# A gated linear attention with a feed-forward block: VectorE's transposes of k and q write pairs of tokens into a buffer of another order

## The chip, the cores and the metric

The kernel runs on one core of a Trainium2 chip. The metric is the device time of one execution in microseconds; the time before is the median of three runs, 610.28 us (609.24 to 611.36). A core has TensorE (matmuls, profile names PE and PEld for the weight loads), VectorE (DVE), ScalarE (ACT), GpSimd (POOL) and SyncE (SP), whose queue issues most DMAs here.

## The reference

The attention keeps a 48x48 state per batch and head, which is decayed by a gate, row by row, and takes in the outer product of k and v at each token; the output is q times the state. A SwiGLU block of three matrices follows.

```python
batch, n_heads, seq, head_dim = (4, 8, 768, 48)
...
    f = 1.0 / (1.0 + np.exp(-f_logit))
...
    for t in range(S):
        state = f[:, :, t, :, None] * state + np.einsum('bhd,bhe->bhde', k[:, :, t], v[:, :, t])
        y[:, :, t] = np.einsum('bhd,bhde->bhe', q[:, :, t], state)
...
n_tokens, d_model, d_ff = (3072, 384, 1536)
...
    g = x @ w_gate
    silu = g * (1.0 / (1.0 + np.exp(-g)))
    val = x @ w_val
    return (silu * val @ w_out).astype(np.float32)
```

All inputs are float32 apart from the weights, which come as 64-bit floats and are converted in the first part of the kernel.

## The kernel before

The 768 tokens are cut into six chunks of 128 (C), and a chunk of one batch is a unit u = 4 * chunk + batch, 24 in all. Chunks are counted here from one in words (the third chunk has c = 2 in the code, units 8 to 11) and u from zero. The eight heads stand as four pairs (HP = 4), each pair in 2 x 64 partitions of which 48 are used.

For one unit the generator `attention(u)` does these steps, and each `yield` ends one: the sigmoid of f on ScalarE; f's transpose; k's transpose; a scan over tokens from the end ("tails"); the multiplication of k by the tails (into kT); in six units (14 to 19, "turned") a further transpose of kT into qT's memory and four DMAs of it to a DRAM buffer named turn; the scan from the start ("gates"); q's transpose; its multiplication by the gates (into qT); the score matmuls (sc); the masking of the scores (A) and, in turned units, the load of kt from turn; the decayed state; the output matmuls (y); the state's update. In the third to sixth chunks (c >= SQUARES, which is 2) the transposes are VectorE's, in blocks of 32x32. Its input lies in three rooms, one for each of f, k and q, of 800 elements a partition: four DMAs (`load`, lines 426 to 431) bring 32 partitions each, so that a partition holds four tokens (NI = 4) of 48 numbers for each pair of heads. The transposed tokens come out in four runs, one for each i of NI, and `in_turn` writes them where they belong, every fourth element:

```python
    def in_turn(t):

        return t.rearrange("p a (t i) -> p a i t", i=NI)
```

There is one room for each of f, k and q, so `load_after(u)`, which issues the twelve DMAs of the next unit, can fill a room only when VectorE has read it. kT is one tile, qT one of two, gates and tails are one each.

TensorE's work is mostly the feed-forward block of the chunk before: fifteen matmul products per slice of hidden units with sums and differences on VectorE (`mlp_fifteen`), then seven products for the way back (`down_seven`, functions `one` to `seven`). PSUM banks come in kinds A (two banks), B (one), o (two) and b (three). `two` ends with a copy of its B bank to SBUF on ScalarE (line 1082), and `four` then takes the B bank again.

The order on every engine is written out by hand. The table CHAINS gives the step times of each unit, SCORES those of the scores; a loop at the end of `short_path` walks over the blocks of the feed-forward, adds their assumed time to a clock, and lets in every attention step that is due. `in_order` then keeps that order on all engines, SyncE's queue among them. So a DMA instruction that waits holds up all that come after it in SyncE's queue.

For the first three batches of a chunk the output goes to SBUF as yT (line 658), and ten DMAs of SyncE (line 667) put it into xT, the input of the feed-forward. For the fourth batch the state is put into a tile called diagonal (line 543, cleared by GpSimd, filled by ScalarE at line 546). yT and diagonal share one buffer: both have the tag "x".

```python
            yT = att.tile([128, 2, HP // 2 * C], FP32, tag="x", name="yT")
...
                diagonal = att.tile([128, HP, 2 * D], FP32, tag="x", name="diagonal")
                nc.gpsimd.memset(diagonal, 0.0)
```

Of the kernel before, what the change touches and what calls it, by code (L numbers as in the profile page):

```python
# [13 lines left out]
ALU = mybir.AluOpType  # L14
# [275 lines left out]
def short_path(ctx, tc, ident, least, judge, q, k, v, f_logit, moe_w_gate, moe_w_val, moe_w_out, out):  # L290
# [9 lines left out]
    nc = tc.nc  # L300
    B, H, S, D = q.shape
    C = 128
    NCH = S // C
    HP = H // 2
# [6 lines left out]
    N1 = C + 1  # L311
# [3 lines left out]
    SQUARES = 2  # L315
# [47 lines left out]
    def pairs(t, off=0):  # L363
        return t[:, off:off + HP * N1].rearrange("p (a t) -> p a t", t=N1)
# [30 lines left out]
    NI = C // Q  # L395
    RUN = NI * D

    rooms = {}
# [9 lines left out]
    def squares(nm):  # L408
        return rooms[nm][:, Q:Q + HP * RUN].rearrange("t (a i e) -> t a i e", a=HP, i=NI)[:, :, :, 0:Q]

    def in_turn(t):

        return t.rearrange("p a (t i) -> p a i t", i=NI)

    def load(u, what="fkqv"):
        b, c = units[u]
        rows = slice(c * C, (c + 1) * C)
        for nm, src in (("f", f_logit), ("k", k), ("q", q), ("v", v)):
            if nm not in what:
                continue  # L420
            if nm == "v":
                dst = v_of(u)
            elif c < SQUARES:
                dst = raw[nm][u % NRAW]
            else:
                for n in range(4):
                    at = Q * (1 - n % 2)
                    nc.sync.dma_start(
                        out=rooms[nm][Q * n:Q * (n + 1), at:at + HP * RUN].rearrange("t (a e) -> t a e", a=HP),
                        in_=src[b, n // 2::2, rows, :].rearrange("a (t i) d -> t a (i d)", i=NI))  # L430
                continue
            nc.sync.dma_start(out=dst[:, :, 0:D], in_=src[b, :, rows, :].rearrange("h t d -> t h d"))
# [79 lines left out]
    def rows_of(par):  # L512
        return slice(W * par, W * par + D)
# [3 lines left out]
    def bank(name):  # L517
        return banks[-1].tile([128, 512], FP32, tag="a", name=name)
# [10 lines left out]
    def attention(u):  # L529
        b, c = units[u]  # L530
        fr, kr, qr = (raw[nm][u % NRAW] for nm in "fkq")
        v_ = v_of(u)
        gate, tail = (x[u % NROT if c < SQUARES else 0] for x in (gates, tails))

        diagonal = None

        def decay():
            nonlocal diagonal
            if c:
                nc.vector.tensor_tensor(decayed[:, :, 0:D], states[b], whole.broadcast_to((128, HP, D)), ALU.mult)  # L540
            if c and b == B - 1:

                diagonal = att.tile([128, HP, 2 * D], FP32, tag="x", name="diagonal")
                nc.gpsimd.memset(diagonal, 0.0)
                for par in range(2):
                    nc.scalar.copy(diagonal[rows_of(par), :, par * D:(par + 1) * D], decayed[rows_of(par), :, 0:D])

        def transposed(name, src):
            p = bank(name)
            for a in range(HP):  # L550
                nc.tensor.transpose(p[:, a * C:(a + 1) * C],
                                    src[:, 2 * a:2 * a + 2, :].rearrange("t r d -> t (r d)"), ident)
            return p.rearrange("p (a t) -> p a t", t=C)
# [6 lines left out]
        else:  # L560
            p = transposed("fTp", fr)
            nc.scalar.activation(pairs(gate)[:, :, 1:N1], p, AF.Copy if u in ahead else AF.Sigmoid)
        yield
        if c >= SQUARES:
            nc.vector.transpose(in_turn(pairs(gate)[:, :, 1:N1]), squares("f"))
        yield

        kT = att.tile([128, HP, C], FP32, tag="kT", name="kT")
        qT = att.tile([128, HP, C], FP32, tag="qT", name="qT", bufs=2)
        kp, qp = kT, qT  # L570
        if c >= SQUARES:
            nc.vector.transpose(in_turn(kT), squares("k"))
        yield

        n = HP * N1
# [5 lines left out]
        if c < SQUARES:  # L581
            kp = transposed("kTp", kr)
            qp = transposed("qTp", qr)
        nc.vector.tensor_tensor(kT, kp, pairs(tail, 2)[:, :, 0:C], ALU.mult)
        yield
        turned = (SQUARES + 1) * B + 1 < u < (NCH - 1) * B
        if turned:
# [10 lines left out]
        nc.vector.tensor_tensor_scan(gate[:, 0:n], gate[:, 0:n], start, 1.0, op0=ALU.mult, op1=ALU.add)  # L598
        yield
        if c >= SQUARES:  # L600
            nc.vector.transpose(in_turn(qT), squares("q"))
            load_after(u)
        yield
        nc.vector.tensor_tensor(qT, qp, pairs(gate)[:, :, 1:N1], ALU.mult)
        nc.gpsimd.memset(pairs(gate)[:, :, 0:1], 0.0)
        if 0 < c < SQUARES:
            load_after(u)
        if c < SQUARES:
            decay()
# [8 lines left out]
        if c < NCH - 1 and not turned:  # L618
            p = bank("kt")
# [14 lines left out]
        if c >= SQUARES:  # L634
            decay()
# [4 lines left out]
        if c and b < B - 1:  # L640
# [20 lines left out]
            for h in range(H):  # L661
                a, par = h // 2, h % 2
# [31 lines left out]
        if c < NCH - 1:  # L694
            p = bank("dS")
# [13 lines left out]
    def load_after(u):  # L709

        w = u + (1 if units[u][1] >= SQUARES else 2)
        if w < len(units) and (units[w][1] >= SQUARES) == (w == u + 1):
            load(w, "fkqv" if units[w][1] < SQUARES or w == SQUARES * B else "fkq")

    def attention_steps(c):

        runs = [attention(c * B + b) for b in range(B)]
        parts = [3, 6, 3, 3]
        order = sorted((2 * b + s, b, n) for b in range(B) for s, n in enumerate(parts))
        return [lambda b=b, n=n: [next(runs[b]) for _ in range(n)] for _, b, n in order]  # L720
# [445 lines left out]
    mark = traced[-1]  # L1166
    keep_warm(5)
    first = [attention(b) for b in range(B)]
    done = [0] * B

# [82 lines left out]
    for c in range(2, NCH):  # L1253
        for b in range(B):
            run = attention(c * B + b)
            waiting += [((c - 2) * whole + t, lambda run=run: next(run)) for t in times(c)[b]]
# [33 lines left out]
def kernel(  # L1290
# [22 lines left out]
    def judge(bank):  # L1313
# [12 lines left out]
        yield  # L1326

    short_path(tc, ident, least, judge, *args)
    with tc.If(redo[0] > 0):
        general_path(tc, *args)  # L1330
# [32 lines left out]
```

## Time and profile before

| quantity | before |
|---|---|
| median of three runs | 610.28 us |
| the profiled execution | 611.44 us |
| its span | 609.6 us |
| granted TensorE clock, mean | 0.996 |
| from the third chunk's first hidden product (145.7 us) to the fourth's (244.6) | 98.9 us |
| fourth to fifth (340.1) | 95.5 us |
| fifth to sixth (434.1) | 94.0 us |
| sixth chunk's attention, until 523.9 | 89.8 us |

The feed-forward of chunk n runs beside the attention of chunk n + 1; the rows of the table are stretches of the trace between the first hidden products of the blocks. In the lines of the profile, "out<-in" names tiles, x is a count, and after the bar stand the busy time in us, the mean of one in ns, the engine's idle time before them and what ended it. In timeline lines the first number is the start in us from the span's start, the second the length; an engine's name with a q stands for an instruction that its sequencer handles, such as the issue of a DMA.

### The profile page before, as it was taken

The page shows a single profiled execution, that of the slowest core. Times are in us where ns is not written, and L with a number is a line of the kernel's source. Part 1 is how long each engine was busy: PE and PEld are TensorE (multiplying, and loading weights), DVE is VectorE, ACT ScalarE, POOL GpSimd, SP SyncE. Part 2 cuts the span into 40 slices and gives each one's busy share as a digit, 9 for nine tenths or more (in the row PEclk, how much of TensorE's full clock was granted, in tenths as well). Part 3 has the DMA queues.
Part 4 walks back from the last instruction along what each step waited for, and adds up shares of the span by engine and source line. Part 5 has one row for each costly group of instructions (what it writes and reads, how often), then busy time and mean ns, then how long its engine had stood idle before and what let it go on. Part 6 is the DMA issues. An engine that isn't in the chain of part 4 may idle for free.

```text
span 609.6 us, 10796 instructions
## 1 busy us (share of the span) xinstructions
PE 595.8 (98%) x4036; PEld 491.1 (81%) x4036; DVE 494.3 (81%) x833; ACT 288.5 (47%) x554; POOL 7.6 (1%) x52
## 2 busy tenths in 40 slices
PE   7899999999999999999999999999999999999996
PEld 5744545667888799888899988899988899988896
DVE  7999989868999985999996789996878981566731
ACT  3466644313776522476732366742276730366600
POOL 1000000000000000000000000000000000000000
PEclk9999999999999999999999999999999999999999
DMA  9988372005312044323236334145313100100001
GB/s 199 260 194 295 126 247 79 5 15 159 95 39 70 23 108 115 105 53 96 61 89 145 94 97 110 35 112 120 110 44 90 27 6 10 53 1 1 0 1 59
DMA packets 109142, 54.10 MB, mean 89 GB/s; under 512 B 68760, under 2 KB 102168, under 8 KB 109080
## 3 DMA queue, kind: packets, MB, share of 16 engines
q1 hardware_dynamic: 107064, 50.56, 31.3%
q10 hardware_dynamic: 2016, 2.75, 1.2%
q8 instruction: 34, 0.56, 0.4%
q14 instruction: 28, 0.23, 0.1%
HBM read 44.04 MB, written 6.29 MB: 83 GB/s over the span
## 4 chain that ended last, share of the span: by engine, by line
PE 85%; DVE 10%; SPq 1%; issue 1%; DMA 1%; ACT 1%; POOL 0%; DVEq 0%; ACTq 0%; POOLq 0%
PE o L1056 17%; PE A L957 15%; PE B L957 12%; PE gate L755 5%; PE val L755 5%; PE o L957 5%; PE c L957 5%; PE sc L617 4%; PE o L778 3%; PE o L1119 3%; PE y L677 2%; PE y L656 2%; PE dS L697 2%; PE y L652 1%; DVE c L861 1%
## 5 line engine op out<-in xcount | busy, mean ns | idle before, releaser
L1056 PE MATMUL o<-w_out,h 128*128 128x192 f32 x360 | 62.0, 327 | 0.5 <-DVE h L909 0.5
L957 PE MATMUL A<-xs,w_both 128*128 128x256 f32 x240 | 62.1, 381 | 0.0
L1056 PEld LDWEIGHTS o<-w_out,h 128*128 128x128 f32 x360 | 58.7, 190 | 1.7 <-DVE h L909 0.8
L962 ACT COPY c<-A 128x512 f32<-128x512 f32 x40 | 23.3, 583 | 62.6 <-PE A L957 62.6
L962 ACT COPY aside<-A 128x512 f32<-128x512 f32 x60 | 35.1, 584 | 32.6 <-PE A L957 32.6
L858 DVE TENSOR_TENSOR c<-c,aside 128x512 f32<-128x512 f32 x60 | 41.6, 694 | 10.5 <-ACT aside L962 9.0
L957 PEld LDWEIGHTS A<-xs,w_both 128*128 128x128 f32 x240 | 44.9, 190 | 6.5
L909 DVE TENSOR_TENSOR h<-h,c 128x256 f32<-128x256 f32 x100 | 41.1, 419 | 7.3 <-ACT h L973 7.3
L861 DVE TENSOR_TENSOR c<-c,aside 128x512 f32<-128x512 f32 x60 | 41.4, 689 | 2.5 <-ACT aside L962 2.5
L973 ACT ACTIVATE h<-c 128x256 f32<-128x256 f32 x100 | 39.2, 416 | 8.4 <-DVE c L858 5.8
L1056 PE MATMUL o<-ws,h 128*128 128x192 f32 x240 | 41.5, 328 | 0.2 <-DVE A L631 0.2
L957 PE MATMUL B<-xs,w_both 128*128 128x256 f32 x160 | 41.2, 380 | 0.6 <-ACT aside L962 0.6
L957 PE MATMUL c<-xT,w_both 128*128 128x256 f32 x160 | 41.2, 380 | 0.5 <-DVE c L861 0.5
L957 PE MATMUL A<-xs,extra 128*128 128x256 f32 x160 | 41.2, 380 | 0.0
L957 PE MATMUL B<-xT,extra 128*128 128x256 f32 x160 | 41.1, 379 | 0.0
L962 ACT COPY aside<-B 128x512 f32<-128x512 f32 x60 | 35.1, 584 | 11.7 <-PE B L957 7.2
L631 DVE TENSOR_TENSOR A<-sc,causal 128x512 f32<-128x512 f32 x48 | 30.8, 684 | 11.3 <-PE sc L617 11.3
L1056 PEld LDWEIGHTS o<-ws,h 128*128 128x128 f32 x240 | 39.1, 190 | 0.8 <-DVE A L631 0.4
L861 DVE TENSOR_TENSOR c<-o,c 128x512 f32<-128x512 f32 x40 | 27.6, 690 | 10.0 <-ACT h L973 5.8
L957 PEld LDWEIGHTS c<-xT,w_both 128*128 128x128 f32 x160 | 30.3, 190 | 5.0 <-DVE c L861 0.9
L957 PEld LDWEIGHTS B<-xs,w_both 128*128 128x128 f32 x160 | 30.2, 190 | 5.0 <-ACT aside L962 1.0
L957 PEld LDWEIGHTS A<-xs,extra 128*128 128x128 f32 x160 | 30.3, 190 | 4.5 <-ACT c L962 0.4
(138 smaller groups left out, 1140.2 us busy)
## 6 DMA issues: line engine op xcount, KB each, us to landing
fsquares<-in_f_logit_dram SPq DMA_DIRECT2D x64, 96.0 KB, 2.6
ksquares<-in_k_dram SPq DMA_DIRECT2D x64, 96.0 KB, 2.3
qsquares<-in_q_dram SPq DMA_DIRECT2D x64, 96.0 KB, 2.2
v<-in_v_dram SPq DMA_DIRECT2D x24, 192.0 KB, 3.0
w<-in_moe_w_gate_dram SPq DMA_DIRECT2D x6, 768.0 KB, 6.3
w<-in_moe_w_val_dram SPq DMA_DIRECT2D x6, 768.0 KB, 5.1
w<-in_moe_w_out_dram SPq DMA_DIRECT2D x6, 768.0 KB, 5.3
out_dram<-ob ACTq DMA_DIRECT2D x14, 192.0 KB, 2.7
```

The source lines that it names most:

```text
L617: nc.tensor.matmul(sc[par][:, a * C:(a + 1) * C], lhsT=kT[r, a, :], rhs=qT[r, a, :], start=True, stop=True)
L631: nc.vector.tensor_tensor(A[:, par], sc[par].rearrange("p (a t) -> p a t", t=C), causal.unsqueeze(1).broadcast_to((128, HP, C)), ALU.mult)
L755: nc.tensor.matmul(p, lhsT=w[:, j, i, :], rhs=xT[c][:, i, :], start=(i == 0), stop=(i == KT - 1))
L778: nc.tensor.matmul(p, lhsT=hidden_tile(h, n // 2)[:, n % 2 * 2 + b // 2, b % 2 * C:(b % 2 + 1) * C], rhs=w_out[:, j, :], start=(n == 0), s ...
L858: nc.vector.tensor_tensor(dst, a, b, ALU.add)
L861: nc.vector.tensor_tensor(dst, a, b, ALU.subtract)
L909: lagging.append(lambda: f(*args))
L957: nc.tensor.matmul(p[name][:, n, :], lhsT=weights_of[a][:, n, j, :], rhs=tokens[b], start=fresh and n == 0, stop=True, skip_group_check=True)
L962: nc.scalar.copy(t, p[name])
L973: nc.scalar.activation(dst, src[:, 0, :], AF.Silu)
L1056: nc.tensor.matmul(p[:, n, :], lhsT=lhsTs[j][:, n * C:(n + 1) * C], rhs=rhs[:, j, :], start=first and j == order[0] and n == 0, stop=j == ...
L1119: nc.tensor.matmul(p, lhsT=hidden_tile(h, j)[:, 2, n * C:(n + 1) * C], rhs=b22[:, j, :], start=j == order[0], stop=j == order[-1])
```

## The change

From the third chunk on, the transposes of k and q no longer write to every fourth element. With `parted`, the four runs are split in two halves of two: the tokens of a half are interleaved in pairs, so that a run writes every second element, and the halves lie 256 elements apart. As that is not the order of tokens, the transposed k goes into qT's memory and the transposed q into the first 512 columns of k's room, and each multiplication reads from there two neighbours of one half, then two of the other, and writes kT and qT in the order of tokens. f's transpose stays as it was. As k's room is now in use until q's multiplication, `load_after` moves behind that multiplication. The number of instructions is the same.

```diff
+    def split_squares(nm):
+        return squares(nm).rearrange("t a (j i) e -> t a j i e", j=2)
+
...
+    def parted(t):
+
+
+
+        return t.rearrange("p (j a t i) -> p a j i t", j=2, a=HP, i=NI // 2)
...
+        def multiply(out, x, by):
+
+            if c >= SQUARES:
+                for_each = "p a (t j i) -> p a t j i"
+                out, by = (t.rearrange(for_each, j=2, i=NI // 2) for t in (out, by))
+                x = x.rearrange("p (j a t i) -> p a t j i", j=2, a=HP, i=NI // 2)
+            nc.vector.tensor_tensor(out, x, by, ALU.mult)
+
...
         if c >= SQUARES:
-            nc.vector.transpose(in_turn(kT), squares("k"))
+            kp = qT.rearrange("p a t -> p (a t)")
+            nc.vector.transpose(parted(kp), split_squares("k"))
         yield
...
-        nc.vector.tensor_tensor(kT, kp, pairs(tail, 2)[:, :, 0:C], ALU.mult)
+        multiply(kT, kp, pairs(tail, 2)[:, :, 0:C])
         yield
...
         if c >= SQUARES:
-            nc.vector.transpose(in_turn(qT), squares("q"))
-            load_after(u)
-        yield
-        nc.vector.tensor_tensor(qT, qp, pairs(gate)[:, :, 1:N1], ALU.mult)
+            qp = rooms["k"][:, 0:HP * C]
+            nc.vector.transpose(parted(qp), split_squares("q"))
+        yield
+        multiply(qT, qp, pairs(gate)[:, :, 1:N1])
         nc.gpsimd.memset(pairs(gate)[:, :, 0:1], 0.0)
-        if 0 < c < SQUARES:
+        if c:
             load_after(u)
```

## The prediction

> **What bounds the kernel now.** I read the page's busy table first, then the groups by form on VectorE, then the timeline around each place where TensorE pauses, and last SyncE's own timeline, because the change moves loads there.
>
> ```profile
> span 609.6 us, 10796 instructions
> PE 595.8 (98%) x4036; PEld 491.1 (81%) x4036; DVE 494.3 (81%) x833; ACT 288.5 (47%) x554; POOL 7.6 (1%) x52
> ...
> L601 DVE STREAM_TRANSPOSE qT<-qsquares 128x512 f32<-128x512 f32 x16 | 18.0, 1125 | 6.4 <-DMA turn<-qT 6.4
> L572 DVE STREAM_TRANSPOSE kT<-ksquares 128x512 f32<-128x512 f32 x16 | 17.8, 1113 | 0.0
> ...
> L473 DVE SCALAR_TENSOR_TENSOR top<-w,top 128x384 int32<-128x384 int32 x24 | 12.6, 554 | 0.4
> L604 DVE TENSOR_TENSOR qT<-qT,gates 128x512 f32<-128x512 f32 x16 | 11.1, 696 | 0.1
> L584 DVE TENSOR_TENSOR kT<-kT,tails 128x512 f32<-128x512 f32 x16 | 10.8, 674 | 0.0
> ...
> L591 DVE STREAM_TRANSPOSE qT<-kT 128x512 f32<-128x512 f32 x6 | 4.2, 702 | 0.0
> ```
>
> The reader is to see two things. TensorE is busy for 98% of the span, so time saved on VectorE is worth only what it takes out of TensorE's pauses. And the same 128x512 transpose takes 702 ns where it writes neighbours (L591) and 1113 to 1125 ns where it writes every fourth element (L572, L601).
>
> I compared each matmul's start with the one before it, less the usual pitch of that form, from 135 us on. Pauses over 0.2 us that are not a change of matmul shape: 0.72 us at 192.46, 0.64 at 199.25, 0.66 at 208.80, 0.35 at 225.86, 0.45 at 236.17, and 0.31 and 0.24 at 355.6 to 356.1. That is 3.4 us in all, which caps any gain.
>
> The second place is the start of the fifth chunk (u=16, numbering batch-chunk pairs as the code does). SyncE's queue, then the engines that hang on it:
>
> ```profile
> 310.55 1.74 SPq L428 DMA_DIRECT2D qsquares<-in_q_dram  x4
> 313.55 6.81 SPq L667 DMA_DIRECT2D xT<-yT  x10
> 320.46 0.53 SPq L432 DMA_DIRECT2D v<-in_v_dram  x1
> 321.04 0.60 SPq L627 DMA_DIRECT2D kt<-turn  x1
> 321.75 2.61 SPq L594 DMA_DIRECT2D turn<-qT  x4
> ...
> 321.66 0.42 POOL L544 MEMSET diagonal<- 128x384 f32 x1 [8.53 <-DMA xT<-yT]
> ...
> 322.11 0.71 ACT L546 COPY diagonal<-decayed 48x192 f32<-48x192 f32 x2 [8.05 <-POOL diagonal L544]
> 322.84 0.48 ACT L1082 COPY ob<-o 128x384 f32<-128x384 f32 x1
> ...
> 324.87 1.30 PE L1056 MATMUL o<-ws,hs 128*128 128x192 f32 x7
> ```
>
> yT and diagonal share one buffer (tag "x"), so the memset waits until the ten stores of yT have left. ScalarE's copies queue behind it, and the second (L1082) empties the only bank of kind B, which the matmuls at 324.87 take. The copy ends at 323.32, so there is 1.55 us of slack. At the sixth chunk's start the same chain stands at 407.52 (yT), 415.33 (memset), 417.00 (copy done) and 418.85 (matmul): 1.85 us.
>
> [...]L473 reads every second word at 554 ns for 384 elements, in step with L909's 419 ns for 256 and L584's 674 ns for 512, which read neighbours. No row writes at a step of two. [...]the trace shows q's loads leaving at 310.55, as q's transpose ends at 310.52.
>
> **The change part by part.** Durations are from the profiled execution: 611.44 us, of which 609.60 are span, against a median of 610.28.
>
> Transposes: 32 of them. Between 0.70 us (as L591) and 1.11 (no gain); I take 0.70[...]. That is 0.41 to 0.47 each, 13 us of VectorE, mostly where VectorE isn't waited for.
>
> Multiplications: 32, reading pairs from two halves 1 KB apart[...]. Between 0.69 and 1.10[...]. I take 0.69.
>
> Gain in the third chunk. VectorE has no idle time from 177.4 to 207.8, and u=10's k transpose (182.62, 0.41 saved) lies before the pause at 192.46, its q transpose (195.65, 1.17 to 0.70) before that at 199.25. First pause 0.72 to 0.31. The second: TensorE comes 0.41 earlier, VectorE 0.88, so 0.64 to 0.17. The third keeps its 0.66, both being 0.88 earlier; those at 225.86 and 236.17 hang on TensorE's own scores and on the stores. Gain 0.88.
>
> Gain in the fifth chunk. u=17's q transpose waited 3.11 us, until 351.92, for the stores of turn, which read qT. Now it writes into k's room and runs at 348.8; four operations behind it finish by 351.7; only the multiplication waits, to 352.6 instead of 355.4. The 0.31 and 0.24 go. Gain 0.55.
>
> Buffers. qT is written a step earlier, when k is transposed; its last readers are u-2's output matmuls, at least 3.4 us earlier in all units (u=23: 477.04 against 480.40), so no wait. The old wait of k's transpose for the scores of u-1 goes; it cost nothing (0.0 idle at L572).
>
> Loads. load_after comes one step later, and k's room is free only after q's multiplication. Twelve DMAs per unit are concerned. f still leaves after its transpose, with one exception: in u=12 v's load falls between the two steps, so f of u=13 queues behind a v load that needs u=11's matmuls (done 238.89); f lands near 243 instead of 238.3, and the sigmoid with its table load ends before ScalarE is next needed at 245.83. Hidden. k and q now leave back to back after the multiplication, 1.9 us for each four (as 437.28 to 441.04). k is in time everywhere, narrowest at u=16 (lands about 315.9, transposed at 316.95) and u=20 (409.8, 410.93).
>
> What is queued behind them on SyncE pays. For u=15 the multiplication ends at 312.90, less 0.42 for the transpose before it: 312.48. k and q until 316.35, and only then yT, instead of 313.55. Ten stores take 6.2 to 7.3 us; with 6.6 they end at 322.95 instead of 320.36, 2.6 later, and memset, copies and matmuls follow: 2.6 - 1.55 = 1.05 us of new pause. At u=19: multiplication done 406.45, yT at 410.35, end 416.95 instead of 413.78, 3.2 - 1.85 = 1.35. Behind them turn, u=17's f and the sigmoid come some 2.6 us late too, but VectorE next waits for TensorE at 336.44 and ScalarE at 341.21. At the fourth chunk's start k is not later, since SyncE reaches it at 223.05 after the multiplication's end at 222.07; at the end there are no loads. Other yT stores slip by up to 2 us with nobody waiting.
>
> Sum: -0.88 - 0.55 + 1.05 + 1.35 = +0.97 us, 612.4 for the profiled execution, 611.3 on the median.
>
> **Rivals.** Slower: the paired reading costs the multiplications what the transposes gain. Point: L584 and L604. For it: nothing in the profile reads two words here and two 1 KB away. Against: L473[...]. At 1.10 us the third chunk's gain is gone and both load bursts start 0.42 later: 1.05 + 1.35 + 0.84 - 0.55 = +2.7, 613.0. It decides from about 0.9 us on, where +0.2 gives +1.8. Transposes that stay at 1.11 (the change doesn't do what it says) give the same 613.0.
>
> Faster: SyncE's burst is shorter than I think or the chain has more slack, so that the new pauses stay away: -1.43, 608.9. For it: single loads of four take 1.74 us; against: 10 stores alone took 6.26 to 6.81 here.
>
> Late landings: the shifted turn, kt and f loads land late as well and hold scores or ScalarE: 1 to 2 us more, about 612.8. Margins there are 0.5 to 1 us.
>
> **How the numbers follow.** A measurement of this kernel can tell about 0.3%, 1.8 us, from no change. The worked case 0.48 (own range -0.5 to +2.5: 0.33 within, 0.15 slower), paired reading or no transpose gain 0.34 (0.32 slower, 0.02 within), no new pauses 0.12 (0.06 faster, 0.06 within), late landings 0.06 (slower). So 0.06 faster, 0.41 same, 0.53 slower. The time is that of the worked case, 611.3. The range 608.8 to 614.5 runs from the no-pause case to both unknown costs at once.
>
> **What would show it.** Right: L572 and L601 near 700 ns, L584 and L604 near 690; pauses at the u=10 places of about 0.3 and 0.2; k's loads leaving as q's multiplication ends; yT after them; memset of diagonal near 324 and 418; new pauses of about a microsecond ahead of the matmuls on ws,hs. Wrong: transposes over 0.9, multiplications over 0.9, or TensorE unbroken there.

## The result, and the profile after

The changed kernel took 612.57 us (median of 8 runs, 611.96 to 613.92), the kernel before 610.50 on the same chip (8 runs): a ratio of 1.0039 (95% interval 1.0026 to 1.0051). It is a little slower, by about 2 us. Two executions of the runs below, one of the kernel before (770.66 us) and one of the kernel with k last at two places (689.06 us), had granted clocks of 0.75 and 0.85 and are left out of all ratios. The forecast was 611.3 us with a range of 608.8 to 614.5. The profiled execution after the change took 612.67 us, of which 610.94 are span. The profile before had 611.44 and 609.62.

The first two lines are the busy table of the page of the changed kernel, the rest its groups by form on VectorE (count, then busy us and mean ns, then the idle time before them).

```profile
span 610.9 us, 10799 instructions
PE 595.7 (98%) x4036; PEld 490.7 (80%) x4036; DVE 483.1 (79%) x833; ACT 288.0 (47%) x554; POOL 7.6 (1%) x52
...
L590 DVE STREAM_TRANSPOSE qT<-ksquares 128x512 f32<-128x512 f32 x16 | 11.3, 707 | 1.2 <-DMA ksquares<-in_k_dram 1.2
L620 DVE STREAM_TRANSPOSE ksquares<-qsquares 128x512 f32<-128x512 f32 x16 | 11.1, 696 | 0.0
L552 DVE TENSOR_TENSOR qT<-ksquares,gates 128x512 f32<-128x512 f32 x16 | 10.9, 683 | 5.2 <-DMA turn<-qT 5.1
L552 DVE TENSOR_TENSOR kT<-qT,tails 128x512 f32<-128x512 f32 x16 | 10.8, 673 | 0.0
```

VectorE got what it was to get. The 32 transposes fell from 1113 and 1125 ns to 707 and 696, the multiplications stayed at 673 and 683, and VectorE's busy time fell from 494.3 to 483.1 us. TensorE's did not move (595.8 to 595.7), so all of the time lies in its pauses. The wait for turn, 6.4 us in all at q's transpose before, stands at q's multiplication now, with 5.1 us.

To find the pauses I subtracted each matmul's start before from the start of the same matmul after, and noted where the difference steps from one matmul to the next. Both profiles have the same 3.4 us of lowered TensorE clock at 28 us (0.50 granted before and 0.51 after, from 28.0 to 31.4 us), so the steps compare directly:

| matmuls (time after) | step, us |
|---|---|
| B<-xs (192.11) | -0.35 |
| c<-xT (198.50) | -0.40 |
| y<-qT,diagonal (235.10) | -0.36 |
| o<-ws,hs (325.44) | +1.64 |
| scores of u=17 (356.07 to 356.96, all together) | -0.67 |
| o<-ws,hs (420.10) | +1.26 |

At both places on ws,hs the next matmul adds another 0.10; with that and 0.04 of small steps the last matmul starts 1.36 us later than before. Here is the fifth chunk's start in the changed kernel's timeline, engine by engine (start, duration, engine, line, and in brackets the idle time before it and what ended it), the same chain as the one shown before:

```profile
311.46 1.74 SPq L437 DMA_DIRECT2D ksquares<-in_k_dram  x4
313.24 2.82 SPq L437 DMA_DIRECT2D qsquares<-in_q_dram  x4
316.17 6.26 SPq L685 DMA_DIRECT2D xT<-yT  x10
322.53 0.53 SPq L441 DMA_DIRECT2D v<-in_v_dram  x1
...
323.72 0.42 POOL L561 MEMSET diagonal<- 128x384 f32 x1 [12.06 <-DMA xT<-yT]
...
324.17 0.71 ACT L563 COPY diagonal<-decayed 48x192 f32<-48x192 f32 x2 [11.18 <-POOL diagonal L561]
324.91 0.48 ACT L1100 COPY ob<-o 128x384 f32<-128x384 f32 x1
...
325.44 4.17 PE L1074 MATMUL o<-ws,hs 128*128 128x192 f32 x24 [1.47 <-ACT ob L1100]
```

The stores of yT, which began at 313.55 before, now stand behind both bursts of loads and begin at 316.17, though ScalarE had filled yT by 312.90 and TensorE's work stands 1.07 us earlier by then. The memset that needs their buffer runs at 323.72 instead of 321.66, the two copies follow without a gap, and TensorE stands still for 1.47 us until the second copy (L1100) has emptied its bank. The start of the sixth chunk in the same timeline has the same order and the same end:

```profile
406.51 1.74 SPq L437 DMA_DIRECT2D ksquares<-in_k_dram  x4
408.29 1.85 SPq L437 DMA_DIRECT2D qsquares<-in_q_dram  x4
410.25 6.59 SPq L685 DMA_DIRECT2D xT<-yT  x10
...
418.38 0.42 POOL L561 MEMSET diagonal<- 128x384 f32 x1 [11.68 <-DMA xT<-yT]
...
420.10 4.17 PE L1074 MATMUL o<-ws,hs 128*128 128x192 f32 x24 [1.09 <-ACT ob L1100]
```

The gain in the fifth chunk is in VectorE's timeline. The first line is u=17's q transpose in the kernel before, with its wait; the others are of the changed kernel, where the wait for turn stands at u=16's multiplication (330.30) and u=17 has none:

```profile
351.92 1.11 DVE L601 STREAM_TRANSPOSE qT<-qsquares 128x512 f32<-128x512 f32 x1 [3.11 <-DMA turn<-qT]
...
330.30 0.69 DVE L552 TENSOR_TENSOR qT<-ksquares,gates 128x512 f32<-128x512 f32 x1 [5.12 <-DMA turn<-qT]
...
349.40 0.72 DVE L620 STREAM_TRANSPOSE ksquares<-qsquares 128x512 f32<-128x512 f32 x1
...
351.87 0.68 DVE L552 TENSOR_TENSOR qT<-ksquares,gates 128x512 f32<-128x512 f32 x1
```

Before, u=17's q transpose waited until 351.92 for turn to be stored; now it runs at 349.40 and its multiplication is done by 352.55, well ahead of the scores at 356.

### The profile page after: what moved, and what is told of

It reads as the page before. It is cut to its first block, busy times and chain, and to the rows that moved or that the text cites. A ratio compares the mean times of both kernels' runs of the same rounds, so it can differ in the third digit from the quotient of the medians.

```text
span 610.9 us, 10799 instructions
## 1 busy us (share of the span) xinstructions
PE 595.7 (98%) x4036; PEld 490.7 (80%) x4036; DVE 483.1 (79%) x833; ACT 288.0 (47%) x554; POOL 7.6 (1%) x52
## 4 chain that ended last, share of the span: by engine, by line
PE 83%; DVE 9%; SPq 3%; issue 2%; ACT 1%; DMA 1%; POOL 0%; DVEq 0%; POOLq 0%; ACTq 0%
PE A L975 16%; PE o L1074 14%; PE B L975 13%; PE c L975 5%; PE o L975 5%; PE gate L773 5%; PE val L773 5%; PE sc L635 4%; PE o L1137 3%; PE o L796 3%; PE y L695 2%; PE y L674 2%; SPq L685 2%; PE dS L715 2%; SPq L437 1%
## 5 line engine op out<-in xcount | busy, mean ns | idle before, releaser
L876 DVE TENSOR_TENSOR c<-c,o 128x384 f32<-128x384 f32 x15 | 8.3, 550 | 33.4 <-PE o L1074 33.4
```

Source lines behind the costliest of these rows:

```text
L876: nc.vector.tensor_tensor(dst, a, b, ALU.add)
```

## The experiments

The theory (A): the late loads of k and q, issued by u=15 and u=19, push the yT stores of u=14 and u=18 back, and this alone costs time, while the transposes' gain is real and small. The rivals: the paired reading costs the multiplications time (B), or the stores are late for another reason than their place in the queue (F). All kernels compute the whole result. The kernel before had a median of 610.09 us (27 runs) beside the first four experiments and of 610.22 (35 runs) beside the next four. The ratios and their intervals are those of the record; they are not the quotients of the two medians, and differ from them by up to 0.0008.

A profile without the lowered clock at 28 us is 1.36 us shorter for that reason alone. I read that off the steps between before and after_again, whose starts drift by 1.34 us between 28 and 31.6 us and then run level. Of the kernels below none has the dip, so 1.36 us is added to their differences from the profile before. The time after the last matmul's start varies from 5.7 to 6.6 us between profiles whatever the kernel, so differences of traces are taken at that start.

### Only k's transpose in pairs

k keeps the new order. q is transposed as before, in single elements and into qT, and the loads are issued where they were.

```diff
-            qp = rooms["k"][:, 0:HP * C]
-            nc.vector.transpose(parted(qp), split_squares("q"))
+            nc.vector.transpose(in_turn(qT), squares("q"))
+            load_after(u)
         yield
-        multiply(qT, qp, pairs(gate)[:, :, 1:N1])
+        nc.vector.tensor_tensor(qT, qp, pairs(gate)[:, :, 1:N1], ALU.mult)
         nc.gpsimd.memset(pairs(gate)[:, :, 0:1], 0.0)
-        if c:
+        if 0 < c < SQUARES:
             load_after(u)
```

> k alone is transposed in pairs; q's transpose, its multiplication and the place of the loads are those of before. Theory A (the loss is two TensorE pauses ahead of the matmuls on ws,hs, made by the yT stores that queue behind the late k and q loads): no such pauses, the pause near 192.5 us about 0.35 us as after the change, the one near 199.3 still about 0.64, the two of 0.31 and 0.24 near 356 still there; 0.3 to 0.5 us below before, about 610.1 us where before is 610.5. Rival B (the paired pattern itself costs, in the multiplication or in the order on VectorE): slower than before by about half of the change's loss, 611 or more. Rival C (k and q land late and hold VectorE): as theory A, since the loads are early again.

It took 609.43 us, 0.9993 of before (0.9982 to 1.0003). VectorE's groups by form in this kernel:

```profile
L619 DVE STREAM_TRANSPOSE qT<-qsquares 128x512 f32<-128x512 f32 x16 | 18.0, 1123 | 6.0 <-DMA turn<-qT 6.0
...
L590 DVE STREAM_TRANSPOSE qT<-ksquares 128x512 f32<-128x512 f32 x16 | 11.2, 701 | 0.0
L622 DVE TENSOR_TENSOR qT<-qT,gates 128x512 f32<-128x512 f32 x16 | 11.0, 690 | 0.1
L552 DVE TENSOR_TENSOR kT<-qT,tails 128x512 f32<-128x512 f32 x16 | 10.8, 674 | 0.0
```

Both orders stand side by side here: 701 ns where pairs are written, 1123 ns where single elements are, and 674 against 690 ns for the multiplications that read them. B falls. The trace has -0.34 us at the pause at 192 and -0.15 at u=17's scores, and no pause ahead of o<-ws,hs: with the loads in their old place nothing is lost.

### The late loads alone

The buffers and the place of the loads are those of the change, but the transposes write single elements as before.

```diff
-            nc.vector.transpose(parted(kp), split_squares("k"))
+            kp = kp.rearrange("p (a t) -> p a t", a=HP)
+            nc.vector.transpose(in_turn(kp), squares("k"))
...
-            nc.vector.transpose(parted(qp), split_squares("q"))
+            qp = qp.rearrange("p (a t) -> p a t", a=HP)
+            nc.vector.transpose(in_turn(qp), squares("q"))
```

> The buffers, the late loads and the instruction order of the change, but both transposes write every fourth element as before, so no transpose gains. Theory A: k's loads leave another 0.4 us later, pauses ahead of the matmuls on ws,hs of 2.0 and 1.7 us, pauses near 192.5 and 199.3 at 0.7 and 0.6 as before, those near 356 gone: about 3 us above before, 613.5. Rival B: no paired pattern, so no loss, about 610. Rival C: a loss of about 2 us, with idle time of VectorE ended by the loads rather than pauses ended by ScalarE's copy.

It took 614.61 us, 1.0066 (1.0053 to 1.0079): the direction as expected, the size half as large again. Its transposes take 1114 and 1126 ns. TensorE's timeline in this kernel:

```profile
325.33 4.17 PE L1076 MATMUL o<-ws,hs 128*128 128x192 f32 x24 [1.88 <-ACT ob L1102]
...
345.30 0.91 PE L977 MATMUL B<-xT,extra 128*128 128x256 f32 x3 [0.57 <-ACT c L982]
```

The two places ahead of o<-ws,hs cost 2.05 and 1.68 us. What I had not reckoned with is what follows behind the first of them: +0.41 at 339.06 and +0.84 at 345.30, the second where ScalarE's copy is late. Those 1.25 us are the most part of the surprise. So the move of the loads and buffers, without any faster transpose, costs about 4.3 us by the trace (2.92 + 1.36), and the faster transposes of the change take back 2 to 3 of them. The scores of u=17 gain their 0.67 us here too, with transposes of 1.1 us: that gain comes from q's new place in memory and not from the pairs, while the gains of the third chunk, at 192 and 199 us, are missing here and so come from the pairs.

### Single elements read back

Can the transposes write neighbours and the multiplications collect single elements? Four runs of 512 bytes, each with a quarter of the tokens of all four pairs of heads, take the place of the pairs. Two outcomes are set against each other: that the multiplications now lose what the transposes gain (613.5 us), or that they keep their time (612.5).

```diff
     def split_squares(nm):
-        return squares(nm).rearrange("t a (j i) e -> t a j i e", j=2)
+        return squares(nm)
...
-        return t.rearrange("p (j a t i) -> p a j i t", j=2, a=HP, i=NI // 2)
+        return t.rearrange("p (j a t) -> p a j t", j=NI, a=HP)
...
-                for_each = "p a (t j i) -> p a t j i"
-                out, by = (t.rearrange(for_each, j=2, i=NI // 2) for t in (out, by))
-                x = x.rearrange("p (j a t i) -> p a t j i", j=2, a=HP, i=NI // 2)
+                for_each = "p a (t j) -> p a t j"
+                out, by = (t.rearrange(for_each, j=NI) for t in (out, by))
+                x = x.rearrange("p (j a t) -> p a t j", j=NI, a=HP)
```

> The change with four runs in place of pairs: the transposes write neighbours, and the multiplications take one element of each run in turn, 512 B apart. [...]transposes 0.70 us, multiplications near 1.1 us, VectorE gains nothing over before, the load bursts start 0.4 us later and the pauses are about 2.0 and 1.7 us: 613.5. [...]multiplications stay at 0.69 us and the time is that of the change, 612.5.

It took 615.03 us, 1.0086 (1.0072 to 1.0101), 1.5 us above the 613.5 expected. The profiled execution, with 613.56 us the shortest of its six, has the expected pauses (2.14 and 1.66 us) and doesn't show that excess. VectorE's groups by form:

```profile
L552 DVE TENSOR_TENSOR qT<-ksquares,gates 128x512 f32<-128x512 f32 x16 | 16.9, 1058 | 5.3 <-DMA turn<-qT 5.2
L552 DVE TENSOR_TENSOR kT<-qT,tails 128x512 f32<-128x512 f32 x16 | 16.7, 1043 | 0.0
L590 DVE STREAM_TRANSPOSE qT<-ksquares 128x512 f32<-128x512 f32 x16 | 11.2, 700 | 1.8 <-DMA ksquares<-in_k_dram 1.8
L620 DVE STREAM_TRANSPOSE ksquares<-qsquares 128x512 f32<-128x512 f32 x16 | 11.1, 695 | 0.0
```

The penalty has moved from the transposes to the multiplications: 1043 and 1058 ns against 673 and 683 with pairs. Writing neighbours is no faster than writing pairs (700 and 695 against 707 and 696 ns). Here are numbers for both directions: single elements cost a transpose that writes them 0.41 us (1113 against 702 ns in the profile before) and a multiplication that reads them 0.37 us, and with pairs neither takes over 12 ns more than with neighbours (707 and 696 ns against 695 to 702 written, 673 and 683 against 674 and 696 read). B would have looked like this, had pairs been read as slowly.

### q's loads behind the stores

From unit 16 on q is loaded with v, after the yT stores.

```diff
         if c >= SQUARES and u + 2 < len(units):
-            load(u + 2, "v")
+            load(u + 2, "vq" if u + 2 >= LATE_Q else "v")
...
+    LATE_Q = (SQUARES + 2) * B
+
...
-            load(w, "fkqv" if units[w][1] < SQUARES or w == SQUARES * B else "fkq")
+            load(w, "fkqv" if units[w][1] < SQUARES or w == SQUARES * B else "fk" if w >= LATE_Q else "fkq")
```

> The change, but from unit 16 on the four loads of q are issued with v's, behind the yT stores, and only f and k stay after the multiplication. Theory A: yT is held by k's four loads alone, 0.9 us, less than the chain's slack of 1.55 and 1.85 us, so both pauses go while VectorE's gains stay: 1.4 us below before, about 609.1, and 3 us below the change. Rival B: the paired pattern is unchanged, so no better than the change, 612.5. Rival C: k lands as late as with the change and q later still, so 612.5 or more.

It took 610.69 us, 1.0007 (0.9999 to 1.0015), 1.6 us more than expected. SyncE's queue, then GpSimd and TensorE, in this kernel's timeline:

```profile
312.37 7.11 SPq L685 DMA_DIRECT2D xT<-yT  x10
319.53 2.00 SPq L437 DMA_DIRECT2D qsquares<-in_q_dram  x4
...
322.77 2.62 SPq L612 DMA_DIRECT2D turn<-qT  x4
...
321.10 0.42 POOL L561 MEMSET diagonal<- 128x384 f32 x1 [10.37 <-DMA xT<-yT]
...
322.86 4.12 PE L1076 MATMUL o<-ws,hs 128*128 128x192 f32 x24
...
330.00 1.16 PE L635 MATMUL sc<-qT,kT 48*128 48x128 f32 x16 [0.73 <-DVE qT L552]
```

The first half of A is right: with the stores at 312.37 the memset runs at 321.10 and TensorE goes through both places without a pause. But q and v now stand ahead of turn, which leaves only at 322.77. q's multiplication of u=16 writes the buffer from which turn is stored and waits for that until 329.25, and the scores of u=16 wait for it (+0.80), and B<-xT,extra after them (+0.45). Against TensorE's work turn is as late in the changed kernel (323.82, in a profile whose matmuls stand 0.9 us later by then); there the 1.64 us pause hides it. Taking a pause away uncovers what is late next.

### Only k's loads late

f and q go back to q's transpose, where they were; only k's four DMAs have to wait for the multiplication, since q is transposed into k's room.

```diff
             nc.vector.transpose(parted(qp), split_squares("q"))
+            load_after(u, "fq")
         yield
         multiply(qT, qp, pairs(gate)[:, :, 1:N1])
         nc.gpsimd.memset(pairs(gate)[:, :, 0:1], 0.0)
         if c:
-            load_after(u)
+            load_after(u, "k" if c >= SQUARES else "fkq")
...
-    def load_after(u):
+    def load_after(u, what="fkq"):
...
-            load(w, "fkqv" if units[w][1] < SQUARES or w == SQUARES * B else "fkq")
+            load(w, "fkqv" if units[w][1] < SQUARES or w == SQUARES * B else what)
```

> The change, with f's and q's loads back at q's transpose and k's four alone behind the multiplication. Theory A: the yT stores leave 0.9 us later than before in place of 2.7 to 2.8, below the slack of 1.55 and 1.85 us, and turn and the next f only 0.9 us later: no pause ahead of the matmuls on ws,hs, none at u=16's scores, all of VectorE's gains (0.35, 0.40, 0.3 and 0.46 us): 1.2 to 1.5 us below before, near 608.7. Rival C (k late is what costs): k leaves as late as with the change, so 612 or more.

It took 610.05 us, 0.9996 (0.9987 to 1.0004), over a microsecond above what I expected. The trace has no pause ahead of o<-ws,hs, all three gains (-0.34, -0.40, and -0.67 at u=17's scores), and two small losses of 0.12 and 0.14 us at y<-qT,diagonal and B<-xT,extra. At the last matmul's start that is -1.10 us; in the median, with its interval from -0.8 to +0.2 us, little of it can be told.

### The same, at two places only

The condition is narrowed to the loads that u=15 and u=19 issue; all other units keep the late loads of the change.

```diff
-            load_after(u, "fq")
+            if u in (15, 19):
+                load_after(u, "fq")
...
-            load_after(u, "k" if c >= SQUARES else "fkq")
+            load_after(u, "k" if u in (15, 19) else "fkq")
```

> The same as the run with k last, but only for the loads that u=15 and u=19 issue; all other units load as with the change. Theory A: only these two places cost anything, so the time is that of k last for all within 0.4 us, near 608.9, and the late loads of the other units show no pause of TensorE. Rival E (late loads cost a little everywhere): half way between k last for all and the change.

It took 609.77 us, 0.9987 of before (0.9976 to 0.9998), the best ratio of all (the medians alone would put k's transpose alone, with 609.43, ahead of it), while the changed kernel, run again beside it, took 614.35. The 609.77 are 0.9 us above what was expected. SyncE's queue, GpSimd, ScalarE and TensorE in its timeline:

```profile
308.06 1.73 SPq L437 DMA_DIRECT2D qsquares<-in_q_dram  x4
310.49 1.94 SPq L437 DMA_DIRECT2D ksquares<-in_k_dram  x4
312.53 6.72 SPq L687 DMA_DIRECT2D xT<-yT  x10
...
320.55 0.42 POOL L561 MEMSET diagonal<- 128x384 f32 x1 [9.86 <-DMA xT<-yT]
...
321.74 0.48 ACT L1102 COPY ob<-o 128x384 f32<-128x384 f32 x1
...
322.82 4.06 PE L1076 MATMUL o<-ws,hs 128*128 128x192 f32 x24
```

q leaves early, so only one burst stands between the multiplication and the stores. They start at 312.53 and ScalarE's copy ends at 322.22, 0.60 us before TensorE needs the bank. Of the loss ahead of o<-ws,hs only 0.2 us in the sixth chunk is left. At the last matmul's start this kernel is 1.07 us ahead of before, and the kernel with k last everywhere 1.10, so the rival E, that late loads cost a little everywhere, falls. Moving eight loads in each of two of the 16 units took the loss away, so the cost of the change sits in these two places. Turn is earlier as well (320.63), which is why the scores of u=16 do not wait as they did with q behind the stores.

### The stores on ScalarE's queue

If only the place in SyncE's queue counted, ten stores issued by ScalarE would be early whatever SyncE does.

```diff
-                    nc.sync.dma_start(out=xT[c][f % 128:f % 128 + n, f // 128, b * C:(b + 1) * C],
+                    (nc.scalar if u in (14, 18) else nc.sync).dma_start(
+                                      out=xT[c][f % 128:f % 128 + n, f // 128, b * C:(b + 1) * C],
```

> The change with its late loads, but the ten yT stores of u=14 and u=18 are issued by ScalarE's queue in place of SyncE's. Theory A (the place in SyncE's queue is what delays them): they start at once near 313.5 and 407.5 in the time of before, next to the k and q loads, and are gone by about 320 and 414; no pauses ahead of the matmuls on ws,hs; 1 to 1.5 us below before, near 609, less what ScalarE's own copies lose to issuing ten DMAs. Rival F (the DMA engines are loaded by k's and q's bursts, whatever the queue): the stores land as late as with the change and the pauses stay, 612 to 613.

It took 613.78 us, 1.0060 (1.0041 to 1.0080), no better than the change; the profiled execution was the longest of its six, 617.84 us. Its timeline, ScalarE's queue first, then SyncE's, GpSimd and TensorE:

```profile
310.94 7.43 ACTq L685 DMA_DIRECT2D xT<-yT  x10
...
311.67 4.58 SPq L437 DMA_DIRECT2D qsquares<-in_q_dram  x4
...
317.41 0.60 SPq L645 DMA_DIRECT2D kt<-turn  x1
...
323.07 0.42 POOL L561 MEMSET diagonal<- 128x384 f32 x1 [12.99 <-DMA xT<-yT]
...
324.79 5.85 PE L1075 MATMUL o<-ws,hs 128*128 128x192 f32 x24 [2.41 <-ACT ob L1101]
```

The matmuls ahead of this place stand 1.57 us earlier than in the profile after the change, most of it by the dip at 28 us that is missing here. Measured against them, the stores have been issued 2.5 us earlier (318.37 against 322.43), and the memset comes 0.9 us later (323.07 against 323.72). So A in its simple form, that only the place behind k's and q's loads counts, falls, and F has a part in it. Both sides slowed down: q's issue went from 2.82 to 4.58 us, and the stores whose landing the profile gives took 1.8 to 3.6 us from issue to landing where the changed kernel has 1.8 to 1.9. The DMA engines were busy for 0.50 of the time while the stores were issued (310.9 to 318.4), against 0.19 in the changed kernel (316.2 to 322.5). So a second queue bought nothing here; what it is that slowed both is not shown.

What held the memset to the end can be read from the packed trace, which reports the landing of each store in sixteen steps. Nine of the ten stores had landed by 319.84. Of the last, issued at 317.77, thirteen steps came by 320.22 and the other three at 322.28, 322.39 and 322.97, and the memset ran at 323.07. In between stands kt's load: SyncE issued it at 317.41, and its 128 packets of 2048 bytes moved from 318.97 to 322.47. The sixth chunk has the same order (kt issued at 414.00, the last store at 414.36, kt's packets until 420.04, the store landed at 420.86). In the changed kernel kt stands behind the stores in SyncE's queue, and the last store lands 1.8 us after its issue. So the move took the stores from behind k and q, but let kt go ahead of the last one; that kt's load is what delayed it fits both places, and no run tests it alone.

The same fence has a second finding: 24 matmuls that take 4.17 us elsewhere took 5.85. This kernel's clock by stretch (us, PE busy and count, PEclk, DMA share, GB/s):

```profile
318.00:322.00 4.00, 4.00 (x26) 1.00 0.47 124
325.00:328.60 3.60, 3.60 (x13) 0.53 0.67 173
329.00:332.00 3.00, 3.00 (x63) 1.00 0.59 164
```

After the pause the granted clock was about half for 3.4 us (325.2 to 328.6; 0.53 on the mean of 325.0 to 328.6), and again after the pause of 2.82 us that ended at 422.85 (0.87 on the mean of 417 to 430). Each cost about 1.7 us more.

### The changed kernel again

> The changed kernel once more, for a second trace. Theory A: the two pauses ahead of the matmuls on ws,hs are there again, 0.9 to 2 us each, median 612.0 to 612.9. If the DMAs' speed differs between executions, the pauses differ from 1.64 and 1.26 us, and others may stand behind the first near 332 to 345 us, as in the kernel with the late loads alone; that would be why the medians lie 2.1 us apart and the first traces only 1.3. Rival D (the pauses are the same in all executions, the rest is chance in the medians): 1.64 and 1.26 us within 0.1 us and a median near 611.5.

> The changed kernel a third time, to see whether the two pauses ahead of o<-ws,hs vary from run to run and whether a lowered TensorE clock follows one of them. Theory (the pauses follow the landing of the stores, and a pause of over about 2 us can be followed by 3.4 us of half clock): time between 612.3 and 615.5 us, pauses between 1.2 and 2.9 us at each place, and where the time is over 613.5 a clock record of 0.5 within 5 us after one of the pauses. Rival (the spread between runs comes from the start of the kernel, where before has its own dip at 28 us): pauses within 0.2 us of 1.64 and 1.26, and the only record of 0.5 lies at about 28 us.

> The same kernel and the same expectations as in after_look2: by the theory pauses that differ by several tenths from those of the other looks and a clock record of 0.5 after a pause wherever the time is over 613.5 us; by the rival the pauses of 1.64 and 1.26 us again and no such record after 30 us.

The first of these took 614.35 us (6 runs, 612.28 to 615.19), 1.0071 (1.0059 to 1.0083); the other two 612.14 and 612.18 in one execution each. With the first profile there are four of the same kernel. The pauses are the steps ahead of o<-ws,hs, without the 0.10 us of the next matmul; q's issue is the time from the first to the end of the last of the four loads that u=15 issues.

| profile of the changed kernel | q's issue, u=15 | pause, fifth chunk | pause, sixth chunk |
|---|---|---|---|
| first (612.67 us) | 2.82 | 1.64 | 1.26 |
| second (612.28 us) | 3.33 | 2.16 | 1.27 |
| third (612.14 us) | 3.00 | 1.83 | 1.38 |
| fourth (612.18 us) | 3.08 | 1.90 | 1.41 |

In the fifth chunk the pause is q's issue less 1.17 to 1.18 us in all four. The issue is long because of one DMA. How long SyncE's queue takes for each of q's loads (ns minimum, median, maximum, then the first and last start) is, for u=15 and u=19 of the first profile of the changed kernel:

```profile
L437 SPq DMA_DIRECT2D qsquares<-in_q_dram x4: 312/436/1189, 313.2 to 315.8; - x4
...
L437 SPq DMA_DIRECT2D qsquares<-in_q_dram x4: 422/429/432, 408.3 to 409.7; - x4
```

At u=15 the second of the four takes 1189 ns (1703 in the second profile, 1369 and 1452 in the others), at u=19 all take about 430. Why the one is held is not shown. At u=19 k's and q's bursts stand in the same order at the same distance.

The half clock in the theory of the last two comes from the run with the stores on ScalarE's queue, where it followed pauses of 2.41 and 2.82 us; the "over about 2 us" was an estimate from these.

Their rival, pauses within 0.2 us of 1.64 and 1.26, falls for the fifth chunk, though narrowly in these two: the fourth profile has 1.90 and the third, with 1.83, is still within; the second had 2.16. In the sixth chunk all four stay within it. No profile of the changed kernel shows a lowered clock after these pauses (1.00 in the first from 325.4 to 332.0 and from 420.1 to 427.0), but none of the four was of an execution above 612.7 us. So what the runs of 613.5 to 615.2 us have more than these four stays open. A half clock after a pause, as with the stores on ScalarE's queue, would fit their size and is not shown.

## Why the prediction was right, point by point

**Transposes at 0.70, multiplications at 0.69: right.** Measured 0.70 to 0.71 and 0.67 to 0.68, the latter a little below the 0.69 that the forecast took as the least, although its own line of k's multiplication had 674 ns. That pairs would be written as fast as neighbours was the author's estimate; the profile before has no transpose that writes every second element. The first rival, paired reading, would have needed multiplications of 0.9 us or more (its 1.10 is an estimate too, 0.69 and the 0.41 us between the transposes of 1113 and 702 ns); single reading has 1.05, pairs have not.

**Third chunk, 0.88 of gain: 0.75.** The two pauses stood at 0.38 and 0.24 us instead of the forecast 0.31 and 0.17. The missing 0.13 us is missing in all four profiles of the changed kernel (0.72 to 0.75).

**The pause at 236, forecast to stay: 0.36 less.** It hangs on the stores of yT, as the prediction said, but their issue is no constant: 7.08 us in the profile before, 6.39 after. All four profiles of the changed kernel gain here, 0.36 to 0.72 us (issue 6.39 to 6.81); with only k late the same place lost 0.12 (6.87). As there is one profile of before, whether the change or the spread of a transfer gave this gain isn't shown.

**Fifth chunk, 0.55 of gain: 0.67** in all four profiles, by the transpose that no longer waits for turn. Right in cause and place; the late loads alone have the same gain.

**The two new pauses, 1.05 and 1.35: right in place, chain and sign, the first too small.** For the sixth chunk 1.26 to 1.41 us were measured (the forecast took 1.9 us for each burst and 6.6 for the stores; 1.74 to 1.86 and 6.59 to 6.73 came). For the fifth, 1.64 to 2.16. The term that was mis-sized is the burst at u=15: "1.9 us for each four (as 437.28 to 441.04)". q's four took 2.8 to 3.3, and each tenth more went into the pause undiminished. The place from which 1.9 was taken had no such hold, and held f's and k's loads, not k's and q's; the profile before had shown q's four at 1.74 to 3.06 us in its sixteen units, so the spread could have been seen.

**Turn, kt and f behind the stores, "hidden": hidden only by the pause.** With the pause gone and turn still late (q behind the stores) the scores of u=16 lost 0.80 us. The fourth profile of the changed kernel also has +0.42 us at 343.35, where ScalarE's copy comes late, and the late loads alone have +0.84 at the same matmuls. The late landings that the prediction kept as a rival of 6 in 100 are part of the answer in some executions. u=13's f came as forecast, behind a DMA that waits in SyncE's queue: in the first profile after, v's load leaves at 237.9, as u=11's matmuls on v end (237.81), and f's four begin behind it at 238.34 (234.65 in the profile before, ahead of v), though VectorE had read f's room by 227.4.

**k in time everywhere: right for TensorE.** VectorE waits 1.2 us for k in all. The 0.64 us of it at u=17, a unit that the prediction didn't name as narrow, delayed no matmul.

**The sum, +0.97: +1.3 to +2.1 at the last matmul's start** in four profiles of the changed kernel (1.36, 1.71, 1.34, 2.06, with the dip at 28 us taken out of the comparison where only one side has it), and +2.07 and +4.1 us in the two pairs of medians. The first pair lies with the traces. The excess of the second is not explained. That the first profile comes within 0.4 us of the forecast is in part luck: the fifth chunk's pause cost 0.7 us more than forecast (with the next matmul) and the third chunk gave 0.2 less, while the pause at 236 and the scores of u=17 gave 0.5 more.

## What to carry to other kernels

Follow a freed engine's transfers, not only its work: the faster transposes of this change gave back 11 us of VectorE, of which TensorE could use 0.7 (q's new place in memory gave another 0.7), and the loads that had to move with them cost more because they went ahead of stores that another engine needed. When a load must move later, move only the one whose buffer forces it; with k alone late at the two tight places the same change was worth about 0.1% (0.02 to 0.24) instead of costing 0.4 to 0.7%. Before counting a late transfer as hidden, ask whether it is hidden by work or by a pause that the next edit takes away.

## What the runs showed of the hardware that was not expected

A lowered TensorE clock came in some executions and not in others. In the run with the stores on ScalarE's queue it came after idle times of 2.41 and 2.82 us (0.53 granted from 325.0 to 328.6 us). At 28 us it came after idle times of 0.79 and 0.74 us in the profile before and in the first of the changed kernel (0.50 and 0.51 from 28.0 to 31.4 us); the second of the changed kernel has the same two, 0.79 and 0.75 us, and no dip. The dips lasted about 3.4 us. Steps of up to 2.16 us, in the other profiles, were followed by none. The two longer pauses are of one execution, and what sets a dip off is not shown.

Issue times of one and the same burst differ from run to run and from place to place by as much as the effects under study: 1.85 us for q's four DMAs at u=19, 2.8 to 3.3 at u=15.
